# A written-out instruction schedule for attention plus gated MLP: a planner that counts DMA lanes and port locks, a new order of the first steps, and four fp32 matmul passes replaced by GpSimd subtractions

## The chip, the cores and the metric

One core of one Trainium2 chip runs the whole program. The metric is device time in microseconds (us). Five engines work side by side: TensorE (PE, with its weight loads PEld), VectorE (DVE), ScalarE (ACT), GpSimd (POOL) and SyncE (SP), which here only issues DMAs.

## The reference, cut to what matters

```python
# attention within chunks of 64 tokens; B, H, S, D = 8, 8, 576, 64
scores = (q_c @ k_c^T) / 8 ; attn = exp(scores - max) ; attn /= sum(attn) + 1e-9
x = (attn @ v_c), heads side by side            # (8, 576, 512), fp32
# gated MLP
h = gelu_tanh(x @ w_in)                         # w_in is 512 x 1024
u, v = h[..., :512], h[..., 512:]
v_n = (v - mean(v)) / sqrt(var(v) + 1e-6) * g_ln
v_s = einsum('ts,bsd->btd', w_sg, v_n) + b_sg   # over the 576 tokens
out = x + (u * v_s) @ w_out                     # w_out is 512 x 512
```

`w_in` and `w_out` arrive as float64 values, each as two 32-bit words, and are turned into fp32 pairs on the chip.

## The kernel before, in words

Every large product is done in three fp32r passes: each operand is split into a high part (rounded to fp32r) and a low part (what the rounding left), and low x high, high x low and high x high are added up in PSUM. So each weight and each activation passes through a split: a copy to the high part on ACT and a subtraction for the low part on DVE or POOL.

The work goes by batch (8) in units. `v_unit(b, m)` makes 128 tokens of v (12 matmuls of 512 columns), then gelu on ACT, statistics on DVE, the power -0.5 on POOL, and the split of the normalized v. `u_unit(b, dt)` makes 128 columns of u (24 matmuls of 288 columns). `s_unit` mixes tokens by w_sg and multiplies by u. The output product is `o_unit` in the first two batches and `o_fast` (seven half-size products) from batch 2 on. Between these stand the attention tiles (128 tokens each): `att_scores` (steps S and P), `att_transpose` (T), `att_out` (O and Q); the tiles below 5 go by `first_scores` and `first_out`.

The weights are prepared at the start. A quarter of `w_in` (512 columns of words) is loaded by `v_w_load` or `u_w_load` (steps L and, from within, w), taken apart by `pair_begin` (steps W and X: mostly DVE bit operations) and made into a high and a low part by `pair_end` (steps w and x). `pair_end` writes the high part with ACT, then adds in PSUM four passes over 512 columns: the fp32 value times an fp32 identity, two bf16 passes with the remaining bits of the float64 value, and the high part times the fp32r identity; ACT copies the sum to the low part. `w_out` is prepared in eight pieces of 256 columns by `o_w` (steps Y): `double_begin` has two two-input operations (multiply, add) by the engine `pick("Z")`, `double_end` one subtraction by `pick("Y")`. `pick(step)` gives GpSimd where the name is in `ON_POOL`, VectorE otherwise. The same tuple says, as `l0` to `l3`, for which of the first attention tiles `keep` makes the low part on POOL from a copy in SBUF, rather than on DVE from PSUM.

Nothing is issued where it is written. `Recorder` collects every operation into a `Plan`, so all of them bear line 224 in the profile and have to be told apart by their tiles. `Plan.emit` finds the true dependences, simulates the engines three times with the prices of `Op.price` (`run`; due times from `due`), and then issues every operation in the order of the planned start times. Each engine executes its own list strictly in order. TensorE may be planned out of the written order within a window of 96 operations (`AHEAD`); other engines take, of what can start within 200 ns, what is due first. The string `START` is the written order for batches 0 and 1 and for all weights; a letter is a step and the number its tile. It sets which TensorE work stands first, and by that all due times. Four scratch buffers of the tag `tmp` are shared by `hs`, `blocks`, `ot` and `r`, so an `ot` that waits for its output DMA can hold up any of the others.

Of the kernel before, what the change touches and what calls it, by code (L numbers as in the profile page):

```python
# [11 lines left out]
F32 = mybir.dt.float32  # L12
# [6 lines left out]
ALU = mybir.AluOpType  # L19
# [4 lines left out]
P = 128  # L24
DM = 512
DF = 1024
DH = DF // 2
# [15 lines left out]


START = """
L0 A0 B0 A1 B1 L1 S0 L2 T0 D11 A2 W0 A3 W1 L3 A4 S1 W2 S2 w0 w1 W3 T1 O0 w2 S3 O1 T2 w3 D14 O2 T3 S4 M0 v00 X0 O3 G0 T4
v01 A8 B8 O4 x0 X1 v02 x1 X2 v03 X3 v04 U0 x2 g0 g1 U1 x3 g2 g3 g4 F0 u02 F1 P5 u03 T5 s00 T6 P7 s01 Q5 s02 T7 T8
s03 Q7 v10 v11 Y0 v12 Y1 v13 Y2 u10 Y3 u11 Y4 u12 Y5 Y6 u13 Y7 A10 B10 s10 s11 P9 A12 s12 s13 T9 o00 T10 P11 A14
o01 o02 o03 Q9 B12 T11 o10 T12 o11 Q11 B14 S13 A15 o12 T13 o13
"""  # L50

SUMS = {5: 0, 6: 1, 7: 2, 8: 3}
# [14 lines left out]
}  # L67


ON_POOL = ("l0", "l1", "l2", "l3", "n2")  # L70
ACT_SOFTMAX = (0, 2, 4)


# [5 lines left out]
G_BLOCK = {(0, 0): 0, (1, 0): 1, (1, 1): 2, (0, 1): 3}  # L79


ENGINES = ("tensor", "vector", "scalar", "gpsimd", "sync")
AHEAD = 96
WAIT = {"tensor": 100, "gpsimd": 120}
# [33 lines left out]
class Op:  # L118
    def __init__(self, engine, method, args, kwargs):
        self.engine, self.method, self.args, self.kwargs = engine, method, args, kwargs  # L120
        outs = [kwargs["out"] if "out" in kwargs else args[0]]
        ins = [a for a in (*args[("out" not in kwargs):], *kwargs.values()) if is_ap(a)]
        ins = [a for a in ins if a is not kwargs.get("out") and a is not kwargs.get("accum_out")]
        self.outs, self.ins = outs + [a for a in [kwargs.get("accum_out")] if a is not None], ins
        self.deps, self.succ, self.tiles = set(), [], []
        self.table = next((TABLES.get(f, 0) for f in (*args, *kwargs.values()) if isinstance(f, AF)), 0) if engine == "scalar" else 0
        self.cost, self.lag = self.price()

    def price(self):

        n = max(a.free_size() for a in self.outs[:1] + self.ins[:2])
        psum = any(a.space == PSUM for a in self.outs + self.ins)
        if self.engine == "tensor":
            x = self.ins[-1]
            n = self.outs[0].free_size()
            if x.dtype == F32R:
                return 4.6 + 0.447 * n, 160
            if x.dtype == BF16:
                return 4.6 + 0.42 * n, 160
            if self.ins[0].ap[0][1] == D:  # L140
                return 39, 160
            return (115 if self.method == "transpose" else 1.76 * n + 10), 160
        if self.engine == "sync":
            size = self.ins[0].size() * 4
            return (460 if self.ins[0].ap[-1][1] >= P else 640), 2000 + size / 400
        if self.engine == "vector":
            one = len(self.ins) == 1 and not psum and self.method in ("tensor_copy", "tensor_scalar")
            return 75 + (0.53 if one else 1.04) * n, 80
        if self.engine == "scalar":
            return 100 + 0.82 * n + (100 if len(self.outs) > 1 else 0), 100  # L150
        return (850 if "pow" in str(self.kwargs.get("op")) else 200 + 1.8 * n), 42
# [10 lines left out]
class Plan:  # L162
# [82 lines left out]
    def run(self, users, after, at):  # L245
        ops = self.ops
        late = self.due(users, after, at)
        left = [len(op.deps) for op in ops]
        ready = [0.0] * len(ops)
        done = [None] * len(ops)  # L250
        start = [None] * len(ops)
        free = dict.fromkeys(ENGINES, 0.0)
        count = {t: len(u) for t, u in users.items()}
        gone = dict.fromkeys(users, 0.0)
        slots = {key: [0.0] * n for key, n in self.room.items()}
        key_of = self.tag_of
        tensor = [k for k, op in enumerate(ops) if op.engine == "tensor"]
        pe, table, wire = 0, 0, 0.0
        open_ = {e: {k for k, op in enumerate(ops) if op.engine == e and not left[k]} for e in ENGINES}

        def begin(k):
            op = ops[k]
            if left[k]:
                return None
            t = ready[k]
            for name in op.tiles:
                if count[name] < len(users[name]):
                    continue
                key = key_of[name]
                rank = 0 if name == next(n for n in self.order[key] if count[n] == len(users[n])) else 1  # L270
                if len(slots[key]) <= rank:
                    return None
                t = max(t, sorted(slots[key])[rank] + WAIT.get(op.engine, 33))
            return max(t, free[op.engine])

        for _ in range(len(ops)):
            best = None
            for e in ENGINES:
                if e == "tensor":
                    while pe < len(tensor) and start[tensor[pe]] is not None:  # L280
                        pe += 1
                    ks = [k for k in tensor[pe : pe + AHEAD] if start[k] is None]
                else:
                    ks = open_[e]
                found = [(b, k) for k in ks if (b := begin(k)) is not None]
                if not found:
                    continue
                t0 = min(found)[0]
                if e == "tensor":
                    t, k = min(found)  # L290
                    if best is None or t < best[0]:
                        best = (t, k)
                    continue
                t, k = min(
                    (late[k] + (1300 if ops[k].table not in (0, table) else 0), b, k) for b, k in found if b <= t0 + 200
                )[1:]
                if best is None or t < best[0]:
                    best = (t, k)
            t, k = best
            op = ops[k]  # L300
            e = op.engine
            if e != "tensor":
                open_[e].discard(k)
            start[k] = t
            cost = op.cost
            if e == "scalar" and op.table not in (0, table):
                table = op.table
                cost += 1200
            free[e] = t + cost
            done[k] = t + cost + op.lag  # L310
            if e == "sync":
                wire = max(t + 2000, wire) + op.lag - 2000
                done[k] = wire
            for name in op.tiles:
                if count[name] == len(users[name]):
                    slots[key_of[name]].remove(min(slots[key_of[name]]))
                count[name] -= 1
                gone[name] = max(gone[name], done[k])
                if not count[name]:
                    slots[key_of[name]].append(gone[name])  # L320
            for s in op.succ:
                left[s] -= 1
                if e != "tensor" or ops[s].engine != e:
                    ready[s] = max(ready[s], done[k] + WAIT.get(ops[s].engine, 33))
                if not left[s] and ops[s].engine != "tensor":
                    open_[ops[s].engine].add(s)
        return start
# [14 lines left out]
def block_attention_gated_mlp(ctx: ExitStack, tc: tile.TileContext, qkv, w_in, w_out, w_sg, g_ln, b_sg, out):  # L342
    nc = Plan(tc.nc)
# [25 lines left out]
    ident_r = const.tile([P, P], F32R, name="ident")  # L369
# [62 lines left out]
        q, lw, top = words[:, :n], words[:, 1::4], p.bitcast(U16)[:, 1::2]  # L432
        nc.vector.scalar_tensor_tensor(q, lw, 9, top, op0=ALU.logical_shift_right, op1=ALU.bitwise_or)

    def pair_end(n, hi, lo, st):

        f = st[:, 2 * n : 3 * n].bitcast(F32)
        p, q = st[:, 3 * n : 4 * n].bitcast(BF16)[:, 1::2], st[:, : 2 * n].bitcast(BF16)[:, :n]
        ps = ps_m.tile([P, 2, 512], F32, name="pm")[:, 0, :n]
        shape = lambda a: a.rearrange("p (k c) -> p k c", k=hi.shape[1]) if len(hi.shape) == 3 else a  # L440
        nc.scalar.mul(hi, shape(f), -1.0)
        terms = [(ident, f), (low[0], q), (low[1], p), (ident_r, hi)]
        for i, (a, c) in enumerate(terms):
            out_ps = shape(ps) if c is hi else ps
            nc.tensor.matmul(out_ps, a, c, start=(i == 0), stop=(i == len(terms) - 1))
        nc.scalar.mul(lo, shape(ps), -1.0)

# [8 lines left out]
        return a.rearrange("p (n k e) -> p n k e", n=n, k=2)  # L456

    staged = {}

    def v_w_begin(kt):  # L460

        pair_begin(DH, staged["v", kt])

    def v_w_end(kt):
        pair_end(DH, win_h[:, kt, DH:], win_l[:, kt, DH:], staged["v", kt])
        u_w_load(kt)

    def v_w_load(kt):
# [11 lines left out]

    def u_w_end(dt):
        cols = slice(dt * P, (dt + 1) * P)
        pair_end(DH, win_h[:, :, cols], win_l[:, :, cols], staged["u", dt])

    def o_w(et, half):
        nonlocal wout_h, wout_l
# [359 lines left out]
    held = {}  # L846
# [250 lines left out]
```

## Time and profile before

| | |
|---|---|
| median of 3 runs | 511.3 us (511.25 to 512.17) |
| profiled execution: time, span | 512.99 us, 511.2 us |
| PE busy | 493.0 us, 96% |
| DVE busy | 390.7 us, 76% |
| ACT busy | 288.8 us, 57% |
| POOL busy | 80.8 us, 16% |

Busy times are shares of the span of one execution. PE's ends are modelled, so a gap between two matmuls shows only where it is longer than the pipeline that the model adds. Times of rows are us from the start of the span, or ns where marked.

### The profile page before, as it was taken

To read this page: it belongs to the slowest core of one execution; us is meant where nothing else is said; L and a number is where in the kernel's file an instruction comes from. 1 tells how busy PE (TensorE), PEld (TensorE's weight loads), DVE (VectorE), ACT (ScalarE), POOL (GpSimd) and SP (SyncE) were. 2 spreads that over 40 slices of the span, in tenths; PEclk is the share of its full clock that TensorE was granted. 3 is DMA by queue.
4 is the path that set the end of the run, shared out by engine and by line. 5 is a ranking of instruction groups with operands and counts; after the bars stand their busy time and mean duration, and the time that the engine had idled before them with its cause. 6 is when DMAs were issued, how large, how long until landed. Compare 5 with 4: busy or idle time off the path is not lost.

```text
span 511.2 us, 12425 instructions
## 1 busy us (share of the span) xinstructions
PE 493.0 (96%) x5201; PEld 453.9 (89%) x5206; DVE 390.7 (76%) x719; ACT 288.8 (57%) x493; POOL 80.8 (16%) x83
## 2 busy tenths in 40 slices
PE   7899999999997989999999999999999999999996
PEld 5667898799987889998999899998999899998996
DVE  6889879898966697698758697698758797577056
ACT  5788667844434868439642578439642578313120
POOL 0122200220510241011200141011200131002000
PEclk9999999999998999999999999999999999999999
DMA  8984011223245422414120504415120501020002
GB/s 330 356 188 150 0 44 42 85 84 124 65 132 161 140 52 74 126 56 136 38 73 25 169 22 108 126 65 138 30 71 24 172 19 27 1 71 24 1 1 92
DMA packets 52683, 46.58 MB, mean 91 GB/s; under 512 B 35218, under 2 KB 45458, under 8 KB 52628
## 3 DMA queue, kind: packets, MB, share of 16 engines
q1 hardware_dynamic: 52628, 45.80, 29.8%
q8 instruction: 41, 0.67, 0.6%
q14 instruction: 14, 0.11, 0.1%
HBM read 36.34 MB, written 9.44 MB: 90 GB/s over the span
## 4 chain that ended last, share of the span: by engine, by line
PE 56%; DVE 24%; ACT 11%; issue 3%; DMA 2%; POOL 1%; SPq 1%; DVEq 0%; POOLq 0%; ACTq 0%
PE pm L224 55%; DVE nmax L224 5%; ACT ptT L224 3%; DVE sm L224 2%; DVE pt L224 2%; DVE st L224 2%; DVE blocks L224 2%; DVE hs L224 2%; ACT L224 2%; ACT z L224 2%; DVE v L224 1%; ACT xf L224 1%; PE banks L224 1%; ACT pt L224 1%; DVE gl L224 1%
## 5 line engine op out<-in xcount | busy, mean ns | idle before, releaser
L224 PE MATMUL pm<-wsg,v 128*128 128x288 f32 x768 | 108.1, 296 | 0.4 <-issue 0.4
L224 PEld LDWEIGHTS pm<-wsg,v 128*128 128x128 f32 x768 | 103.9, 188 | 0.9 <-issue 0.5
L224 ACT COPY ptT<-blocks 32x256 f32<-32x256 f32 (+1 forms) x93 | 44.2, 476 | 34.2 <-DVE blocks L224 32.0
L224 POOL TENSOR_TENSOR sm<-sm,neg_half 128x1 f32<-128x1 f32 x36 | 31.0, 863 | 197.7 <-DVE sm L224 193.5
L224 PE MATMUL pm<-xh,win_l 128*128 128x288 f32 x256 | 55.6, 299 | 0.0
L224 PE MATMUL pm<-xh,win_h 128*128 128x288 f32 x256 | 55.0, 296 | 0.0
L224 PE MATMUL pm<-xl,win_h 128*128 128x288 f32 x256 | 55.0, 296 | 0.0
L224 PE MATMUL pm<-gh,wout 128*128 128x288 f32 x272 | 54.0, 300 | 0.0
L224 PE MATMUL pm<-win_h,xl 128*128 128x512 f32 x128 | 51.7, 404 | 0.0
L224 POOL TENSOR_TENSOR pt<-pt,nmax 128x512 f32<-128x512 f32 x27 | 30.2, 1132 | 131.5 <-DVE nmax L224 126.1
L224 PE MATMUL pm<-win_h,xh 128*128 128x512 f32 x128 | 50.9, 397 | 0.0
L224 PE MATMUL pm<-win_l,xh 128*128 128x512 f32 x128 | 50.7, 396 | 0.0
L224 ACT CAST gh<-u 128x576 fp32r<-128x576 f32 x32 | 21.4, 673 | 48.9 <-DVE u L224 48.8
L224 ACT ACT_TABLE_LOAD x32 | 41.1, 1283 | 9.0 <-DVE pt L224 7.7
L224 PEld LDWEIGHTS pm<-gh,wout 128*128 128x128 f32 x272 | 43.3, 192 | 0.3
L224 DVE TENSOR_TENSOR u<-pm,u 128x576 f32<-128x576 f32 x32 | 24.1, 753 | 24.7 <-PE pm L224 24.5
L224 PEld LDWEIGHTS pm<-xh,win_l 128*128 128x128 f32 x256 | 41.4, 188 | 1.3
L224 PEld LDWEIGHTS pm<-xl,win_h 128*128 128x128 f32 x256 | 41.1, 188 | 0.0
L224 PEld LDWEIGHTS pm<-xh,win_h 128*128 128x128 f32 x256 | 41.0, 188 | 0.0
L224 ACT ACTIVATE hs<-pm 128x512 f32<-128x512 f32 x36 | 21.3, 596 | 27.1 <-PE pm L224 23.0
L224 PE MATMUL pm<-gl,wout 128*128 128x288 f32 x136 | 35.8, 300 | 0.0
L224 DVE BATCH_NORM_STATS2 sm<-hs 128x6 f32<-128x512 f32 x36 | 24.7, 686 | 10.8 <-ACT hs L224 10.7
(126 smaller groups left out, 955.3 us busy)
## 6 DMA issues: line engine op xcount, KB each, us to landing
qk<-qkv SPq DMA_DIRECT2D x31, 512.0 KB, 4.7
out_dram<-ot SPq DMA_DIRECT2D x31, 288.0 KB, 2.2
av<-qkv SPq DMA_DIRECT2D x116, 64.0 KB, 3.3
wsg<-w_in SPq DMA_DIRECT2D x4, 512.0 KB, 7.6
wout<-w_in SPq DMA_DIRECT2D x4, 512.0 KB, 8.0
st<-w_out SPq DMA_DIRECT2D x8, 256.0 KB, 3.0
qkv_w<-qkv SPq DMA_DIRECT2D x2, 768.0 KB
stage<-w_sg SPq DMA_DIRECT2D x5, 288.0 KB, 3.8
```

Of the source, the lines that this page charges most:

```text
L224: getattr(getattr(self.nc, op.engine), op.method)(*op.args, **op.kwargs)
```

## The change

1. `START` is another order of the same steps; among the differences, the loads come as `A1 L2 L0 ...`, `U1` stands before `U0`, the pieces `Y` lie differently among `u1x` and `s1x`, and at the end of batch 1 `Q11` (the attention output of tiles 11 and 12) stands behind `o12 T13` instead of ahead of `B14`.
2. `ON_POOL` becomes `("Y", "Z", "l0", "l2", "l3", "n2")`: the three two-input operations of each of the eight `w_out` pieces move from DVE to POOL, and the low part of attention tile 1 moves from POOL to DVE.
3. `pair_end` gets an engine. For the four u parts of `w_in` (`REST_U = "gggg"`), POOL subtracts the high part from the fp32 value, and the fp32 pass over the identity goes; for the v parts nothing changes.
4. The planner's prices are set anew, a DMA waits for the oldest of eight lanes, and a DVE operation and a POOL operation that both lock are not planned side by side.

```diff
-L0 A0 B0 A1 B1 L1 S0 L2 T0 D11 A2 W0 A3 W1 L3 A4 S1 W2 S2 w0 w1 W3 T1 O0 w2 S3 O1 T2 w3 D14 O2 T3 S4 M0 v00 X0 O3 G0 T4
-v01 A8 B8 O4 x0 X1 v02 x1 X2 v03 X3 v04 U0 x2 g0 g1 U1 x3 g2 g3 g4 F0 u02 F1 P5 u03 T5 s00 T6 P7 s01 Q5 s02 T7 T8
-s03 Q7 v10 v11 Y0 v12 Y1 v13 Y2 u10 Y3 u11 Y4 u12 Y5 Y6 u13 Y7 A10 B10 s10 s11 P9 A12 s12 s13 T9 o00 T10 P11 A14
-o01 o02 o03 Q9 B12 T11 o10 T12 o11 Q11 B14 S13 A15 o12 T13 o13
+A1 L2 L0 A0 B0 B1 L1 S0 T0 A2 A4 W0 A3 D11 W1 L3 S1 W2 S2 S3 w0 w1 W3 T1 O0 w2 O1 T2 w3 D14 T3 S4 M0 O2 v00 X0 O3 G0
+T4 v01 A8 B8 O4 x0 X1 v02 x1 X2 v03 U1 X3 v04 U0 x2 g0 P5 x3 g2 g3 g4 F0 u02 g1 F1 u03 T5 s00 T6 P7 s01 Q5 s02 T7 T8
+s03 Q7 v10 v11 Y0 v12 v13 Y2 Y1 u10 Y3 u11 Y4 s10 Y5 s11 Y6 u13 Y7 u12 A10 B10 s12 P9 A12 s13 T9 T10 o02 P11 A14 o01
+o03 o00 Q9 B12 T11 o10 T12 o11 B14 S13 A15 o12 T13 Q11 o13
-ON_POOL = ("l0", "l1", "l2", "l3", "n2")
+ON_POOL = ("Y", "Z", "l0", "l2", "l3", "n2",)
+REST_V, REST_U = "pppp", "gggg"
...
         if self.engine == "sync":
-            size = self.ins[0].size() * 4
-            return (460 if self.ins[0].ap[-1][1] >= P else 640), 2000 + size / 400
+            return (420 if self.ins[0].ap[-1][1] >= P else 620), 2500 + self.ins[0].size() / 100
+        wide = [a for a in self.ins if a.free_size() > 1]
+        copies = self.method in ("tensor_copy", "tensor_scalar") and n > 1
+        if self.engine == "gpsimd":
+            self.locks = self.method == "tensor_tensor" and n > 8
         if self.engine == "vector":
+            self.locks = not psum and (len(wide) > 1 or copies)
...
+            if op.engine == "sync":
+                t = max(t, lanes[0])
+            if op.locks:
+                a, b = held["gpsimd" if op.engine == "vector" else "vector"]
+                if a <= t < b:
+                    t = b
...
         terms = [(ident, f), (low[0], q), (low[1], p), (ident_r, hi)]
+        if eng is not None:
+            eng.tensor_tensor(lo, shape(f), hi.bitcast(F32), op=ALU.add)
+            terms = [(low[0], q), (low[1], p), (ident_r, lo)]
```

## Rows read from the trace of the kernel before

**Rows 1.** Page, part 1: busy time, share of the span, instructions of each engine.
```profile
PE 493.0 (96%) x5201; PEld 453.9 (89%) x5206; DVE 390.7 (76%) x719; ACT 288.8 (57%) x493; POOL 80.8 (16%) x83
```

**Rows 2.** Busy time by stretch: length, each engine's busy us (instructions), clock, DMA, GB/s.
```profile
0.00:36.00 36.00, 29.24 (x369) 21.55 (x374) 28.74 (x59) 25.58 (x83) 5.60 (x10) 1.00 0.96 308
36.00:66.00 30.00, 30.00 (x267) 24.36 (x265) 25.71 (x50) 22.88 (x41) 6.37 (x7) 1.00 0.23 68
66.00:130.00 64.00, 63.11 (x646) 58.84 (x645) 58.42 (x124) 40.51 (x68) 9.22 (x9) 1.00 0.24 75
130.00:160.00 30.00, 26.15 (x370) 24.86 (x372) 21.89 (x37) 11.37 (x20) 7.79 (x6) 1.00 0.39 119
160.00:226.00 66.00, 64.20 (x740) 59.50 (x733) 52.64 (x95) 42.63 (x63) 12.22 (x13) 0.97 0.33 95
226.00:340.50 114.50, 113.93 (x1268) 107.24 (x1267) 88.72 (x159) 68.00 (x101) 17.90 (x18) 1.00 0.30 84
455.20:511.20 56.00, 51.89 (x354) 49.47 (x352) 27.57 (x47) 12.10 (x19) 3.75 (x4) 1.00 0.11 38
```

**Rows 3.** Waits of PE from 0 to 36: who for whom, us in total, times, longest.
```profile
PE pm L224 <- ACT ident L224: 2.4, 1, 2.4
PE pm L224 <- DVE wout L224: 1.2, 1, 1.2
PE pm L224 <- DVE wsg L224: 1.0, 1, 1.0
PE banks L224 <- ACT first_ptT L224: 0.7, 1, 0.7
PE banks L224 <- ACT xf L224: 0.7, 1, 0.7
PE pm L224 <- DVE first_pts L224: 0.6, 1, 0.6
```

**Rows 4.** Timeline 138 to 160: who waits before the longest pause of PE (in brackets).
```profile
146.16 5.82 SPq L224 DMA_DIRECT2D av<-qkv  x8
...
152.08 2.52 SPq L224 DMA_DIRECT2D out_dram<-ot  x2
...
153.72 0.69 PE L224 MATMUL pm<-qk 64*64 64x64 f32 x32 [1.17 <-DVE xl L224]
...
157.85 0.76 DVE L224 TENSOR_TENSOR ot<-pm,xf 128x576 f32<-128x576 f32 x1 [2.52 <-DMA out_dram<-ot]
...
158.64 0.60 DVE L224 COPY ptT<-blocks 32x256 f32<-32x256 f32 x2
159.02 0.30 PE L224 MATMUL pm<-ptT,av 64*64 64x64 f32 x2 [2.69 <-issue]
```

**Rows 5.** PE by stretches of 3 us there: length, busy (instructions), granted clock.
```profile
156.00:159.00 3.00, 0.33 (x3) 1.00 0.43 81
159.00:162.00 3.00, 2.98 (x40) 0.66 0.84 282
162.00:165.00 3.00, 3.00 (x20) 0.77 0.40 91
165.00:168.00 3.00, 3.00 (x20) 1.00 0.27 101
```

**Rows 6.** Timeline around the last of the four fp32 passes, PE's matmuls: start, us, instructions.
```profile
58.92 0.43 PE L224 MATMUL pm<-xh,win_h 128*128 128x288 f32 x2
...
59.19 1.02 PE L224 MATMUL pm<-wout,ident 128*128 128x512 f32 x2
...
60.05 0.60 PE L224 MATMUL pm<-wout,low 128*128 128x512 bf16 x2
```

**Rows 7.** Timelines: PE, the first of the four passes; DVE, the last part's last bits.
```profile
38.60 1.02 PE L224 MATMUL pm<-wsg,ident 128*128 128x512 f32 x2
...
46.99 0.69 DVE L224 SCALAR_TENSOR_TENSOR wout<-wout 128x512 uint16<-128x512 uint16 x1
```

**Rows 8.** Groups by form: the DVE operations that move, and POOL's and DVE's kinds like them.
```profile
L224 DVE TENSOR_TENSOR st<-st 128x256 f32<-128x256 f32 x16 | 6.7, 422 | 0.4
L224 DVE TENSOR_TENSOR wout<-st,wout 128x256 fp32r<-128x256 f32 x8 | 3.4, 421 | 0.5 <-ACT wout L224 0.5
L224 POOL TENSOR_TENSOR pt<-pt,nmax 128x512 f32<-128x512 f32 x27 | 30.2, 1132 | 131.5 <-DVE nmax L224 126.1 <-ACT hs L224 2.8 <-DVE sm L224 2.7
L224 POOL TENSOR_TENSOR xl<-xf,xh 128x512 fp32r<-128x512 f32 x4 | 5.7, 1420 | 26.0 <-ACT xh L224 26.0
L224 POOL MEMSET eye<- 128x128 f32 x1 | 0.2, 205 | 0.3 <-POOLq L1086 0.3
L224 DVE SCALAR_TENSOR_TENSOR wsg<-wsg 128x512 int32<-128x512 int32 x4 | 2.8, 693 | 0.1
L224 DVE TENSOR_TENSOR xl<-pm,xh 128x512 fp32r<-128x512 f32 x28 | 18.3, 687 | 14.8 <-ACT xf L224 13.4 <-ACT xh L224 1.4
```

**Rows 9.** Timeline, DVE beside POOL: first of eight lengthened DVE operations before 160 us.
```profile
16.75 1.27 POOL L224 TENSOR_TENSOR xl<-xf,xh 128x512 fp32r<-128x512 f32 x1 [15.46 <-ACT xh L224]
16.82 1.75 DVE L224 SCALAR_TENSOR_TENSOR wout<-wout 128x512 int32<-128x512 int32 x1
```

**Rows 10.** Timeline 134.5 to 137, DVE and POOL: the last of the eight.
```profile
135.21 1.81 POOL L224 TENSOR_TENSOR r<-r 128x512 f32<-128x512 f32 x1
135.87 1.29 DVE L224 COPY ptT<-blocks 32x256 f32<-32x256 f32 x1
```

**Rows 11.** Timeline of PE, 28 to 28.6: the first matmul of a v unit.
```profile
28.46 0.50 PE L224 MATMUL pm<-win_h,xl 128*128 128x512 f32 x1
```

More of the change, by code (lines that the diff above doesn't have):

```diff
@@ L126, in __init__ @@
         self.table = next((TABLES.get(f, 0) for f in (*args, *kwargs.values()) if isinstance(f, AF)), 0) if engine == "scalar" else 0
+        self.locks = False
         self.cost, self.lag = self.price()
@@ L136, in price @@
             if x.dtype == F32R:
-                return 4.6 + 0.447 * n, 160
+                return (5.9 if n < 400 else 4.6) + 0.447 * n, 160
             if x.dtype == BF16:
@@ L140, in price @@
             if self.ins[0].ap[0][1] == D:
-                return 39, 160
-            return (115 if self.method == "transpose" else 1.76 * n + 10), 160
+                return 40, 160
+            return (118 if self.method == "transpose" else 1.83 * n + 10), 160
         if self.engine == "sync":
-            size = self.ins[0].size() * 4
-            return (460 if self.ins[0].ap[-1][1] >= P else 640), 2000 + size / 400
+            return (420 if self.ins[0].ap[-1][1] >= P else 620), 2500 + self.ins[0].size() / 100
[3 more added lines that the diff above has]
+            self.locks = self.method == "tensor_tensor" and n > 8
         if self.engine == "vector":
+            if self.method == "memset":
+                return 600, 80
+            self.locks = not psum and (len(wide) > 1 or copies)
             one = len(self.ins) == 1 and not psum and self.method in ("tensor_copy", "tensor_scalar")
@@ L254, in run @@
         gone = dict.fromkeys(users, 0.0)
+        heads = {key: list(names) for key, names in self.order.items()}
         slots = {key: [0.0] * n for key, n in self.room.items()}
@@ L257, in run @@
         tensor = [k for k, op in enumerate(ops) if op.engine == "tensor"]
-        pe, table, wire = 0, 0, 0.0
+        pe, table, wire, lanes = 0, 0, 0.0, [0.0] * 8
+        held = {"vector": [0.0, 0.0], "gpsimd": [0.0, 0.0]}
         open_ = {e: {k for k, op in enumerate(ops) if op.engine == e and not left[k]} for e in ENGINES}
@@ L269, in begin @@
                 key = key_of[name]
-                rank = 0 if name == next(n for n in self.order[key] if count[n] == len(users[n])) else 1
+                rank = 0 if name == heads[key][0] else 1
                 if len(slots[key]) <= rank:
@@ L273, in begin @@
                 t = max(t, sorted(slots[key])[rank] + WAIT.get(op.engine, 33))
-            return max(t, free[op.engine])
+            t = max(t, free[op.engine])
+            if op.engine == "sync":
[4 more added lines that the diff above has]
+                    t = b
+            return t
         for _ in range(len(ops)):
@@ L311, in run @@
             if e == "sync":
-                wire = max(t + 2000, wire) + op.lag - 2000
+                wire = max(t + 2500, wire) + op.lag - 2500
                 done[k] = wire
+                lanes.append(wire)
+                del lanes[0]
+            if op.locks:
+                held[e] = [t, t + cost + op.lag]
             for name in op.tiles:
@@ L316, in run @@
                     slots[key_of[name]].remove(min(slots[key_of[name]]))
+                    heads[key_of[name]].remove(name)
                 count[name] -= 1
@@ L433, in pair_begin, with pair_end @@
         nc.vector.scalar_tensor_tensor(q, lw, 9, top, op0=ALU.logical_shift_right, op1=ALU.bitwise_or)
-    def pair_end(n, hi, lo, st):
+    def pair_end(n, hi, lo, st, eng):
         f = st[:, 2 * n : 3 * n].bitcast(F32)
@@ L442, in pair_end @@
         terms = [(ident, f), (low[0], q), (low[1], p), (ident_r, hi)]
+        if eng is not None:
+            eng.tensor_tensor(lo, shape(f), hi.bitcast(F32), op=ALU.add)
+            terms = [(low[0], q), (low[1], p), (ident_r, lo)]
         for i, (a, c) in enumerate(terms):
-            out_ps = shape(ps) if c is hi else ps
+            out_ps = shape(ps) if c is hi or c is lo else ps
             nc.tensor.matmul(out_ps, a, c, start=(i == 0), stop=(i == len(terms) - 1))
@@ L458, in block_attention_gated_mlp @@
     staged = {}
+    REST = {"p": None, "v": nc.vector, "g": nc.gpsimd}
     def v_w_begin(kt):
@@ L464, in v_w_end @@
     def v_w_end(kt):
-        pair_end(DH, win_h[:, kt, DH:], win_l[:, kt, DH:], staged["v", kt])
+        pair_end(DH, win_h[:, kt, DH:], win_l[:, kt, DH:], staged["v", kt], REST[REST_V[kt]])
         u_w_load(kt)
@@ L482, in u_w_end @@
         cols = slice(dt * P, (dt + 1) * P)
-        pair_end(DH, win_h[:, :, cols], win_l[:, :, cols], staged["u", dt])
+        pair_end(DH, win_h[:, :, cols], win_l[:, :, cols], staged["u", dt], REST[REST_U[dt]])
     def o_w(et, half):
```

## The prediction

> **What bounds the kernel now.** I read the page's busy times first, then busy time by stretch, then the timeline at each stretch where PE is not full. PE is busy for 493.0 of 511.2 us [rows 1], so a gain has to come either from less PE work or from the 18.2 us in which PE stands still. The stretches say where those lie [rows 2]: 6.8 us before 36 us, none from 36 to 66, 0.9 from 66 to 130, 3.9 from 130 to 160, 1.8 from 160 to 226, then 0.6 in 114 us and 4.1 at the end (the last results on their way out, which the change leaves alone). From 226 us on PE sets the pace and a better plan has almost nothing to win; what can move lies in the first 226 us.
>
> In the first 36 us PE waits 2.4 us for the identity, which stays, and 4.2 us in five waits for DVE and ACT work on the first tiles and on the v parts of w_in [rows 3]; the 16 DMA engines are busy for 0.96 of that time [rows 2], so part of this is set by data arriving, and part by DVE, busy for 28.7 of 36 us.
>
> The pause at 159 us is one mechanism that the reader can follow [rows 4]. SP issues eight loads of v tiles in 5.8 us, and two output DMAs stand behind them until 152.08. The `ot` buffers that they empty come free late, so DVE waits 2.52 us with its next `ot` at the head of its list; the half-done `ptT` copies of an attention tile stand behind it on DVE and are done from 158.94 on; PE, which has that tile's output next, starts at 159.02 after 2.69 us. Another 1.17 us goes at 153.72. After the pause the granted clock is 0.66 for 3 us and 0.77 for the next 3, and 1.00 again [rows 5]: in part at the lower level, 1.2 GHz instead of 2.4. That is 3 x 0.34 + 3 x 0.23 = 1.71 us more. The place costs 1.17 + 2.69 + 1.71 = 5.57 us.
>
> **Part 1, the fp32 pass.** An fp32 pass over 512 columns is two matmuls; the last of the four begins at 59.19 and the bf16 pass behind it at 60.05 [rows 6], so it takes 0.86 us of PE's line. The first of the four begins at 38.60 [rows 7]. Four go: 4 x 0.86 = 3.44 us. PE is full from 36 to 66 [rows 2], so this shortens its line by that much there. What takes its place is a POOL subtraction of 512 columns, 1.13 to 1.42 us by kinds of the same width [rows 8], between ACT's high part and the last PE pass. Queued behind it on POOL are the power operations of the v units; for these DVE, then ACT wait. PE has v units of other tiles to do meanwhile, and the bits of the last u part, which DVE finishes 0.69 us after 46.99 [rows 7], waited for a pass at 59.19, so I cost the added latency at nothing; without that cover it is up to 1.42 us for each part, 5.7 in all.
>
> **Part 2, w_out on POOL.** Twenty-four DVE operations of 0.42 us go [rows 8]: 16 x 0.422 + 8 x 0.421 = 10.1 us, in a stretch in which DVE is busy for 58.4 of 64 us [rows 2]. Tile 1's low part comes to DVE for 0.69 us [rows 8]. The trace has no POOL two-input operation of 256 columns. From below half of 1.13, 0.57 us; from above the whole, 1.13. POOL's small memset takes 0.21 [rows 8], so the fixed part can't be large: 0.21 + 0.92 / 2 = 0.67 us, an estimate. So POOL gets 24 x 0.67 = 16.1 us, and four subtractions at 1.42 make 21.8; tile 1's 1.28 leaves it: 20.5 net. POOL itself has room, 15.6 of 94 us busy from 36 to 130 [rows 2].
>
> The price is on DVE. A DVE operation that usually takes 0.69 us [rows 8] took 1.75 when it began 0.07 us after a POOL one of 1.27 [rows 9]: it ran when POOL had ended. Eight DVE operations before 160 us are lengthened this way, the first in [rows 9] and the last in [rows 10], by 7.0 us in all, beside 15 POOL operations of 512 columns with 20.5 us: 0.34 us of DVE for each us of POOL. At that rate the added POOL time costs DVE 0.34 x 20.5 = 7.0 us, and DVE is better off by 10.1 - 0.7 - 7.0 = 2.4 us. The bounds are no waiting (9.4 us better) and all of it (11.1 worse). I take DVE as even for PE's line: its relief lies behind a PE that was full there anyway.
>
> The Trainium skill, page "SBUF — State Buffer", section "SBUF: two separate sides", speaks against this move: it says that VectorE operations with two SBUF inputs and GpSimd operations take one shared pair of ports as an exclusive lock, and the one that comes second is blocked for the whole of the other. The 1.75 us of [rows 9] agrees. By that rule moving work to POOL frees no DVE time where DVE wants the ports at every moment; that is the third rival below, whose sum is the one by this rule at its worst; at the trace's rate it is the forecast's.
>
> **Part 3, the planner and the order.** Q11 now stands behind o12 and T13. That gives PE a whole o unit before the tile whose `ptT` came late: 24 matmuls, at 0.13 us each (the two of 288 columns from 58.92 to 59.19 in [rows 6]) 3.2 us, against the 2.69 it waited [rows 4]. PE also arrives 3.4 us earlier, DVE no later. I take the place at 153 to 163 as gone: -5.57, the half clock with it. At worst nothing of it goes, or another pause of this size stands elsewhere. The DMAs count too: the eight loads still hold SP for 5.8 us, and an output that is made earlier can still be issued behind them. What is late next is the run of DVE and ACT work from 160 to 226, where DVE is busy for 52.6 of 66 us and PE loses 1.8 [rows 2]; with PE earlier I let that loss happen a second time: +1.8. For the start I take 0, between the 4.2 us of waits that a good order could remove [rows 3] and as much again that a bad one could add. New prices alone, in the steady stretch, are worth at most its 0.6 us per 114.
>
> **Sum.** On the profiled execution, 512.99 us (span 511.2 and 1.8 around it): -3.44 - 5.57 + 1.8 + 0 + 0 = -7.2, which makes 505.8. This execution stands 1.7 above the median of the runs, so on that scale 511.3 - 7.2 = 504.1.
>
> **Rivals.**
> - *A wait takes the place of the pass* (no change, 511.3; 510 to 512.5). PE gives up 3.44 us by 66 us and gets them back as a longer wait at 153, because SP's loads and the `ot` buffers set that time. For it: the wait there is on a DMA, not on PE. Against: the steps on both sides of it have been reordered, and that DMA's input is made by PE.
> - *Everything that waits goes* (499.0): also three quarters of the 4.2 us in the start, 3.2, and the 1.8 isn't lost again: 511.3 - 3.44 - 5.57 - 3.2 = 499.1. For it: the lanes are counted where DMA is fullest. Against: what the data rate sets no order removes.
> - *The ports make DVE the bound* (slower, 514). Every added us of POOL blocks DVE: DVE gets 11.1 us more between 36 and 130. Its idle time there is 4.3 + 5.6 = 9.9 us [rows 2], but half of that stands where it waits for PE or ACT; 5 absorbed leave 6.1: 511.3 - 3.44 + 6.1 = 514.0, with the pause at 159 still there. It decides from the point where over 9.4 / 20.5 = 0.46 of POOL's time blocks DVE; it was 0.34. A planner that sees the locks speaks against it, DVE's 58.4 busy us of 64 from 66 to 130 for it. It is what the lock in the Trainium skill's page "SBUF — State Buffer" (section "SBUF: two separate sides") would do at its worst.
> - *The order doesn't do what it says:* PE's window of 96 operations lets the planner put Q11's matmuls where they were. Then only the passes go and the 1.8 isn't lost: 511.3 - 3.4 = 507.9. I count this in the forecast's own range.
>
> **How the numbers follow.** Forecast 0.50 (own range 500.5 to 508.5), no change 0.17, everything 0.15, slower 0.18. A measurement of this kernel tells 0.2%, some 1 us, from no change. Faster: 0.50 + 0.15 and half of the no-change case, 0.08, so 0.73; same 0.08; slower 0.19 with a little of that case. The range takes all of the forecast and most of the no-change and the better case: 498.5 to 512.5.
>
> **What would show it.** Eight PE matmul records fewer; no `wsg,ident` or `wout,ident` row behind 36 us; the S units of batch 0 some 3 us earlier. No PE wait over 1 us and a full clock from 130 to 170. DVE's `st` and `wout` sums gone, and its lengthened operations beside POOL at some 0.34 of POOL's added time. The steady stretch of 114.5 us unchanged. The forecast is wrong if a PE wait of several us stands anywhere between 36 and 226, above all one with a lowered clock behind it, or if the first v unit starts later than before, 28.46 us [rows 11].

## The result, and the profile after

The changed kernel takes 504.5 us (median of 4 runs, 503.9 to 504.6) against 511.7 beside it (511.3 to 512.6): ratio 0.985, 95% interval 0.984 to 0.987, faster by some 7.3 us. Forecast were 504.1 us and a gain of 7.2. The number came out; half of its working did not, as the experiments show, and that the errors cancel is luck.

The page's first part (busy us, share, instructions) and the busy times of the changed kernel by the stretches of [rows 2] (length, busy us per engine, granted clock, DMA, GB/s):

```profile
PE 487.9 (97%) x5198; PEld 451.6 (90%) x5198; DVE 383.6 (76%) x696; ACT 288.5 (57%) x493; POOL 107.1 (21%) x110
```

```profile
0.00:36.00 36.00, 29.03 (x389) 22.03 (x390) 27.57 (x61) 26.38 (x84) 6.41 (x10) 1.00 0.90 306
36.00:66.00 30.00, 27.22 (x224) 22.05 (x223) 28.22 (x49) 20.89 (x38) 12.20 (x10) 0.94 0.30 87
66.00:130.00 64.00, 63.84 (x658) 60.41 (x657) 53.38 (x102) 39.99 (x70) 31.12 (x35) 1.00 0.22 67
130.00:160.00 30.00, 30.00 (x417) 29.07 (x416) 26.25 (x45) 16.04 (x27) 8.52 (x7) 1.00 0.43 136
160.00:226.00 66.00, 65.14 (x795) 59.90 (x797) 51.86 (x94) 43.75 (x65) 11.07 (x11) 1.00 0.33 98
226.00:340.50 114.50, 114.35 (x1306) 107.69 (x1299) 88.23 (x159) 68.41 (x103) 18.23 (x18) 1.00 0.30 84
```

Three things are to be seen beside [rows 2]. From 130 to 160 PE is full, where it lost 3.85 us, and the clock stays at 1.00 through 226. From 36 to 66, where PE was full, it now stands still for 2.78 us, the clock is 0.94 (30 x 0.06 = 1.8 us more), and DVE's busy time has grown from 25.71 to 28.22 of 30. The steady stretch is as before.

So the first matmul of batch 0's S units comes later, not earlier, although four passes less lie ahead of it. PE's timeline of the kernel before, then of the changed one (start, us, instructions):

```profile
68.40 0.83 PE L224 MATMUL pm<-wsg,v 128*128 128x288 f32 x5
```

```profile
70.26 3.35 PE L232 MATMUL pm<-wsg,v 128*128 128x288 f32 x24
```

The waits of PE behind this, 36 to 66 us, and the granted clock around the longer one:

```profile
PE pm L232 <- ACT u L232: 1.9, 1, 1.9
PE pm L232 <- ACT hs L232: 0.8, 1, 0.8
```

```profile
54.00:57.00 3.00, 1.09 (x7) 1.00 0.00 0
57.00:60.00 3.00, 3.00 (x17) 0.60 0.00 0
60.00:63.00 3.00, 3.00 (x71) 0.83 0.00 0
```

Where this pause comes from can be followed on the timelines of POOL, DVE, ACT and PE, here from 49 to 57 us (in brackets: idle time before it, and what ended it):

```profile
49.10 1.55 POOL L232 TENSOR_TENSOR win_l<-wout,win_h 128x512 fp32r<-128x512 f32 x1 [2.38 <-ACT win_h L232]
52.81 2.33 POOL L232 TENSOR_TENSOR sm<-sm,neg_half 128x1 f32<-128x1 f32 x1 [2.16 <-DVE sm L232]
```

```profile
49.39 1.87 DVE L232 TENSOR_TENSOR wsg<-stage,wsg 128x576 fp32r<-128x576 f32 x1
...
52.65 0.74 DVE L232 SCALAR_TENSOR_TENSOR hs<-hs,sm,g_bc 128x512 f32<-128x512 f32 x1
53.31 1.41 DVE L232 TENSOR_TENSOR wsg<-stage,wsg 128x576 fp32r<-128x576 f32 x2
```

```profile
55.17 0.72 ACT L232 ACTIVATE v<-hs,sm 128x512 fp32r<-128x512 f32 x1 [3.72 <-POOL sm L232]
55.80 0.63 ACT L232 ACTIVATE u<-pm 128x576 f32<-128x576 f32 x1
```

```profile
56.48 0.54 PE L232 MATMUL pm<-xh,win_l 128*128 128x288 f32 x2 [1.91 <-ACT u L232]
```

The new POOL subtraction for the last u part starts at 49.10; a w_sg split on DVE, usually 0.75 us, begins 0.29 us later and takes 1.87. All of DVE's list behind it is late, with it the sum that POOL's power operation needs. That operation, on one column, starts at 52.81, beside three DVE operations in a row that each read two tensors of SBUF, and takes 2.33 us where its mean is 0.94: some 1.3 us more than in the other places where it was begun beside such an operation (0.92 to 1.02 between 40 and 66 us), so this wait is the larger part of the pause. ACT has the v scaling that needs it at the head of its list and the first u gelu behind; the gelu empties the PSUM buffer that PE waits for.

### The profile page after: what moved, and what is told of

Same layout as the page of the kernel before. It is cut to its first block, busy times and chain, and to the rows that moved or that the text cites. A ratio compares the mean times of both kernels' runs of the same rounds, so it can differ in the third digit from the quotient of the medians.

```text
span 502.7 us, 12445 instructions
## 1 busy us (share of the span) xinstructions
PE 487.9 (97%) x5198; PEld 451.6 (90%) x5198; DVE 383.6 (76%) x696; ACT 288.5 (57%) x493; POOL 107.1 (21%) x110
## 4 chain that ended last, share of the span: by engine, by line
PE 66%; DVE 16%; ACT 9%; DMA 4%; issue 3%; POOL 1%; SPq 0%; DVEq 0%; POOLq 0%; ACTq 0%
PE pm L232 66%; DMA qk<-qkv 2%; DVE nmax L232 2%; ACT L232 2%; DVE u L232 2%; DVE wsg L232 1%; DVE sm L232 1%; ACT pt L232 1%; DMA wout<-w_in 1%; DVE v L232 1%; DVE xl L232 1%; ACT ptT L232 1%; DVE gl L232 1%; DVE hs L232 1%; DVE wout L232 1%
## 5 line engine op out<-in xcount | busy, mean ns | idle before, releaser
L232 POOL TENSOR_TENSOR sm<-sm,neg_half 128x1 f32<-128x1 f32 x36 | 33.9, 942 | 166.0 <-DVE sm L232 164.8
L232 ACT ACTIVATE v<-hs,sm 128x512 fp32r<-128x512 f32 x32 | 23.0, 723 | 20.1 <-POOL sm L232 15.8
```

Of the source, the lines that this page charges most:

```text
L232: getattr(getattr(self.nc, op.engine), op.method)(*op.args, **op.kwargs)
```

## The experiments

Times stand beside runs of the kernel before on the same chip, where its median was 512.8 to 513.0; a ratio is to those. Each edit is to the changed kernel, or, where it says so, to the kernel before. "Order kept" means that every engine issues its list in the order of the changed kernel's plan, so that only the edit differs; "planned anew" means that the planner made new lists for the edited program.

**The changed kernel itself**, on the chip of the last runs:

> The changed kernel itself, beside the others on one chip. Every theory: the same pause of PE at 54 to 57 us; 504 to 506 us, the ratio to before 0.982 to 0.988.

504.1 us, ratio 0.984 (0.981 to 0.986), with the same pause.

**The four passes put back, order kept.**

```diff
+        if eng is not None:
+            nc.before[len(nc.ops)] = lambda: tc.nc.tensor.matmul(ps, ident, f, start=True, stop=True)
...
+                if k in self.before:
+                    self.before[k]()
```

> The changed kernel with its planned order kept as it is, but for each of the four u parts of w_in one fp32 pass over 512 columns is issued on TensorE again, just ahead of the first bf16 pass, into the same PSUM bank (the bf16 pass overwrites it, so nothing else changes). Theory (the four passes lay on PE's line, 0.86 us each): 504.5 + 3.4 = 507.9 us, 507.2 to 508.6. Rival (the change's new pause of PE at 54 to 57 us, or waits for ACT and POOL before it, take the passes in): 504.5 to 505.5.

503.4 us, ratio 0.982 (0.978 to 0.985): not slower with 3.4 us more of PE work, and below even the rival's times. Its busy times from 36 to 66:

```profile
36.00:66.00 30.00, 29.57 (x241) 22.95 (x237) 28.77 (x50) 22.12 (x44) 10.80 (x10) 1.00 0.30 89
```

The clock stays at 1.00. The total refutes my theory's time, but not all of its mechanism. The four passes, then the power operation with the three DVE operations around it, and PE's start behind its only wait in this stretch:

```profile
39.60 1.02 PE L472 MATMUL pm<-wsg,ident 128*128 128x512 f32 x2
45.19 1.02 PE L472 MATMUL pm<-wsg,ident 128*128 128x512 f32 x2
59.41 1.02 PE L472 MATMUL pm<-wout,ident 128*128 128x512 f32 x2
62.13 1.12 PE L472 MATMUL pm<-wout,ident 128*128 128x512 f32 x2
```

```profile
53.61 0.73 DVE L235 SCALAR_TENSOR_TENSOR hs<-hs,sm,g_bc 128x512 f32<-128x512 f32 x1
53.77 0.99 POOL L235 TENSOR_TENSOR sm<-sm,neg_half 128x1 f32<-128x1 f32 x1 [2.17 <-DVE sm L235]
54.27 1.41 DVE L235 TENSOR_TENSOR wsg<-stage,wsg 128x576 fp32r<-128x576 f32 x2
...
56.11 0.54 PE L235 MATMUL pm<-xh,win_l 128*128 128x288 f32 x2 [0.43 <-ACT u L235]
```

Set against the profile of the changed kernel operation by operation, PE is 0.92 us late before the first pass, from the start, and 1.11 late at the end of its work before the pause: the waits took in all but 0.2 of the first two passes' 1.72 us. The last two, behind the pause, put PE back by 1.8 us, their full price. What pays for that is not the passes' doing as far as the rows show: the power operation takes 0.99 us here and 2.33 in the changed kernel, beside the same three DVE operations and begun as long after the first of them (0.16 us). That is 1.34 of the 1.48 us by which the pause is shorter, and with it the lowered clock is gone, another 1.5 us before the last two passes begin. PE's first S matmul starts at 70.17, against 70.26. So in this run two of the four passes were on the path; why the power operation waits less here is open.

**The passes back, planned anew** (`REST_U = "pppp"`):

> The changed kernel with the four fp32 passes in place of GpSimd's subtractions, planned anew. Theory (between 36 and 66 us VectorE, not PE, sets the pace as soon as the passes go, so they cost nothing): PE full from 36 to 66, no lowered clock there, VectorE's lengthened operations there fewer by some 3.3 us, time within 1 us of the changed kernel or below it, 502.5 to 505.5. Rival (the passes are worth their 3.4 us and only this order's pause hides it): 506.5 to 509.

503.5 us, ratio 0.983 (0.981 to 0.985). PE is full again, though DVE is still busy for 28.63 us of this stretch:

```profile
36.00:66.00 30.00, 29.72 (x239) 23.42 (x238) 28.63 (x50) 22.94 (x40) 8.06 (x8) 1.00 0.30 88
```

DVE's lengthened operations there fall from 4.4 us to 2.5 by their rows, less than the 3.3 expected. The theory's result holds: without the part of the change that removes the passes, the other parts give the whole gain. The power operation took 0.93 us in this run, with no pause of PE behind it, so this run does not tell what the subtractions cost from what that operation's wait costs.

**The subtraction alone, in the kernel before** (four lines of `pair_end`, GpSimd for the u parts):

> The kernel before, planned by its old planner and in its old order, with GpSimd's subtraction in place of the four fp32 passes and nothing else. Theory (at this place the passes are worth their 3.4 us only if no new wait takes them; the pause at 153 to 163 stays as it is): 507.9 to 509.5 us with the pause at 153 still there. Rival (a new pause between 40 and 60 us with a lowered clock takes it all): 511 to 513.

513.0 us, ratio 1.000 (0.997 to 1.003): the rival, at its word. A pause of PE appears at 45 us, with a lowered clock behind it; the one at 153 is shorter but there. PE's waits of over 1 us from 36 to 66 and from 130 to 170, and the clock after the first:

```profile
PE pm L224 <- ACT hs L224: 2.4, 2, 1.8
```

```profile
PE pm L224 <- ACT ptT L224: 1.3, 1, 1.3
PE pm L224 <- DVE xl L224: 1.2, 1, 1.2
```

```profile
47.00:51.00 4.00, 4.00 (x13) 0.57 0.02 4
```

**The subtractions on VectorE, order kept.**

```diff
+                rest = op.engine == "gpsimd" and op.outs[0].tensor.name.startswith("win_l")
-                getattr(getattr(self.nc, op.engine), op.method)(*op.args, **op.kwargs)
+                getattr(getattr(self.nc, "vector" if rest else op.engine), op.method)(*op.args, **op.kwargs)
```

> The changed kernel with its planned order kept, but the four subtractions of the u parts of w_in run on VectorE (0.69 us each, 2.8 in all) at their places in the order. Theory (GpSimd's subtractions cost VectorE more than they spare it: three of them hold up one VectorE operation each by 1.1 us, 3.3 in all, and the last one delays the w_sg splits ahead of the pause): PE's pause at 54 to 57 us is shorter by 0.5 us or more and the clock stays up; 502 to 504. Rival (VectorE is the full engine here and 2.8 us more of it delays all): the pause grows, 505 to 507.

502.2 us, ratio 0.980 (0.978 to 0.983), the fastest version run; on the same chip the changed kernel stood at 504.1, though the two intervals overlap. DVE around the last subtraction (compare 49.10 to 51.26 above), then the power operation, and PE's first clock row after its pause:

```profile
48.69 0.69 DVE L233 TENSOR_TENSOR win_l<-wout,win_h 128x512 fp32r<-128x512 f32 x1
49.30 0.75 DVE L233 TENSOR_TENSOR wsg<-stage,wsg 128x576 fp32r<-128x576 f32 x1
```

```profile
51.66 2.26 POOL L233 TENSOR_TENSOR sm<-sm,neg_half 128x1 f32<-128x1 f32 x1 [6.42 <-DVE sm L233]
```

```profile
56.00:59.00 3.00, 3.00 (x24) 1.00 0.00 0
```

On DVE the subtraction takes 0.69 us and blocks nothing; the pause is 1.27 us in place of 1.91, and the clock stays at 1.00. DVE's lengthened operations from 34 to 66 us fall from 4.4 us to 1.1 by their rows, so 2.8 us of work replace 3.3 of waiting. The power operation still takes 2.26 us: its wait does not need a subtraction on POOL. Of the 2.0 us much is the clock: the mean granted clock was 1.000 in the four executions from 501.9 to 502.3 us, and in two of the changed kernel's six on that chip, which took 502.1 and 503.4 us; its other four had 0.992 to 0.998.

**The same, planned anew** (`REST_U = "vvvv"`):

> The same four subtractions on VectorE, planned anew by the new planner. Theory: as with the order kept, 501.5 to 504, since the planner can also place them. Rival: the new order brings a pause of its own with a lowered clock, 505 to 508.

508.0 us, ratio 0.992 (0.990 to 0.994): the rival. The plan has a pause of its own at 38 us, with a lowered clock:

```profile
PE banks L232 <- DVE first_pts L232: 3.1, 1, 3.1
```

The same edit is worth -2.0 us with one order and +3.8 with another.

**ScalarE's gelu ahead of the v scaling, order kept otherwise** (one operation moved one place):

> The changed kernel with its planned order kept, but on ScalarE the first u gelu of batch 0 stands ahead of the v scaling that it follows in the plan. Theory (PE's pause at 54 to 57 us is ScalarE's list standing behind a power operation on GpSimd that waits for the shared ports): the gelu runs by 55.4, PE waits some 1.1 us less, the clock stays at 1.0, and the time is 501.5 to 503.0 us. Rival (the gelu waits itself, for the w_sg splits on VectorE that free its tile, until 55.5 or later): no change, 504 to 505, the clock lowered again.

503.8 us, ratio 0.983 (0.978 to 0.987): in the theory's clock, but not below its upper end. PE's wait for the gelu shrinks from 1.9 to 0.3 us and the clock stays up from 36 to 66; most of the time then goes to the next wait:

```profile
PE pm L238 <- ACT win_l L238: 1.3, 1, 1.3
...
PE pm L238 <- ACT u L238: 0.3, 1, 0.3
```

From the changed kernel's 504.1 this can't be told apart.

**w_out's operations back on VectorE, order kept** (POOL's two-input operations of 256 columns issue on DVE):

> The changed kernel with its planned order kept, but the 24 two-input operations of 256 columns of the w_out pieces run on VectorE again, each at the same place in the order. Theory (about even for PE: the port lock takes back what VectorE is spared): 504 to 505.5 us, DVE's lengthened operations between 75 and 130 us nearly gone. Rival A (VectorE's relief is what removed the pause of PE at 153 to 163 us): that pause comes back, 508 to 510. Rival B (the ports cost more than the move spares): 502 to 503.5.

507.3 us, ratio 0.989 (0.985 to 0.993): 3 us slower, in rival A's direction but short of its 508 to 510, and in another place: there is no pause at 153 but one at 89 us, behind a DVE list that is too long, with a clock of 0.97 over 66 to 130. Against the second profiled execution of the changed kernel the span is 506.0 to 503.0 us: the 1.5 of this pause and 1.7 of clock.

```profile
PE pm L233 <- DVE ptT L233: 1.5, 1, 1.5
```

**The new GpSimd list alone, in the kernel before:**

> The kernel before with the new list of what runs on GpSimd alone (w_out's two-input operations to GpSimd, tile 1's low part to VectorE), old planner, old order, fp32 passes kept. Theory (VectorE's relief from 65 to 130 us is what removes the pause at 153 to 163 us): no PE wait over 1 us there, 505.5 to 507.5 us. Rival A (the ports take it back): 510 to 513 with the pause in place. Rival B (the pause only moves, earlier or later): 508 to 511.

512.7 us, ratio 0.999 (0.997 to 1.002): rival A's time with rival B's mechanism. From 130 to 170 PE loses 1.12 us, where the kernel before loses 3.85, and no wait there is over 1 us. DVE's busy time from 66 to 130 falls from 58.42 to 48.76 us, but the old plan lets PE pause at 88 us, and the clock is low for the 6 us behind it:

```profile
PE pm L224 <- DVE ptT L224: 2.0, 1, 2.0
```

```profile
90.00:96.00 6.00, 6.00 (x51) 0.50 0.22 63
```

**The old START string:**

> The changed kernel with the old START string, planned anew with the new planner. Theory (Q11 behind o12 and T13 removes the pause of PE at 153 to 163 us, worth 5.6): the pause and its lowered clock are back, 508.5 to 511. Rival A (the planner's DMA lanes and locks remove it): no pause there, 503.5 to 506. Rival B (the order of the first steps also cost the new pause at 54 to 61 us): that one goes with the old string, 4.4 less, and the sum is about even at 504 to 506 with the pause at 153 present.

505.9 us, ratio 0.987 (0.983 to 0.991): rival A. With Q11 in its old place the pause at 153 does not come back, PE being busy for 29.58 us from 130 to 160:

```profile
130.00:160.00 30.00, 29.58 (x410) 28.37 (x409) 22.76 (x39) 13.48 (x23) 8.60 (x8) 1.00 0.44 132
```

**The old planner:**

> The changed kernel with the planner of before (old prices, no DMA lanes, no locks), all else new. Theory (the order string, the passes and the w_out move make the gain; the planner little): 503.5 to 506.5. Rival A (the lanes let the output DMAs go before the v loads, and without them PE's pause near 153 us is back): 508 to 511. Rival B (locks unseen, VectorE is blocked at bad moments between 36 and 130): new PE waits there, 506.5 to 509.

510.6 us, ratio 0.996 (0.993 to 0.998): the planner is worth some 6.4 us in this kernel. No pause at 153 either, but two of over 2 us before it, rival B and at more than its price, each with a lowered clock:

```profile
PE pm L226 <- ACT hs L226: 2.3, 1, 2.3
PE pm L226 <- DVE v L226: 2.1, 1, 2.1
```

```profile
48.00:51.00 3.00, 2.84 (x8) 0.63 0.02 5
113.00:117.00 4.00, 4.00 (x21) 0.58 0.01 2
```

**The new planner alone, in the kernel before:**

> The kernel before with the new planner alone (prices, DMA lanes, locks); old order string, old list for GpSimd, fp32 passes kept. Theory (the planner gives few microseconds in this order, and the pause at 153 is the w_out work's): 509 to 512 us, pause present. Rival (the planner removes the pause by itself): 504.5 to 507, no PE wait over 1 us between 130 and 165.

510.4 us, ratio 0.997 (0.994 to 1.000): the theory's time, the rival's mechanism. From 130 to 170 PE loses 0.55 us and the pause is gone, but 1.7 us are lost at 185, and in the start the clock was 0.91, worth over 3 us. That is not the old string's doing by itself: the run above with the same string and planner had 1.00 there. The two quickest executions, 508.6 and 509.0 us, had a mean clock of 0.997, the others 0.990 to 0.993:

```profile
0.00:36.00 36.00, 28.82 (x346) 20.78 (x347) 26.75 (x56) 24.32 (x68) 5.82 (x10) 0.91 0.87 300
...
130.00:170.00 40.00, 39.45 (x552) 37.00 (x551) 30.25 (x55) 18.89 (x34) 5.66 (x5) 1.00 0.42 126
```

## Why the prediction was right, and where it was not

**The passes, -3.44: wrong.** The work went, the time did not. The step that failed is the one that costs POOL's latency "at nothing" because PE has other v units to do. PE was full from 36 to 66 in [rows 2], but DVE was close behind it, 25.71 of 30, and POOL's subtractions made it 28.22: three of them hold up one DVE operation each by 1.1 us, 3.3 in all. PE waits 2.7 us and pays 1.8 in clock: 4.5 against 3.44. I had this as the first rival, in the wrong place (at 153, not at 54).

How the 4.5 divide is shown in part. With the subtractions on VectorE and the order kept, the pause is 0.64 us shorter. The power operation's long wait is another 1.3 us, and it does not come from subtractions on POOL alone: it took 2.26 us without them, and 0.99 with them in the run with the passes. Of the passes themselves, put back with the order kept, the first two were covered by waits and the last two, 1.8 us, were on PE's line. With the passes planned anew the sum comes out the same, 503.5 against 504.1; the subtractions on VectorE planned anew settle nothing, since that plan has a pause of its own.

**The port lock: near in sum, wrong in place.** I priced 7.0 us of waiting, 0.34 us of DVE for each us of POOL, from all of the first 160 us. Counted by their rows in the same way, DVE's lengthened operations there went from 7.0 to 12.3 us, 5.3 more. But beside the u subtractions it is 3.3 us for 6.1 us of POOL, 0.54, in a stretch in which DVE was busy for 28.22 of 30. The Trainium skill, page "SBUF — State Buffer", section "SBUF: two separate sides", says that the one that comes second is blocked for the whole of the other; DVE's 1.87 us at 49.39 agrees. I had not priced the other direction at all: the power operation's 2.33 us, which goes beyond that sentence, since it sat out three DVE operations and not one.

**The w_out move: even for PE was too low.** With the order kept it is worth 3 us, 1.7 of them the clock. POOL's operations of 256 columns took 0.77 us, estimated at 0.67, in a stretch in which DVE's busy time fell from 58.42 to 53.38:

```profile
L232 POOL TENSOR_TENSOR st<-st 128x256 f32<-128x256 f32 x16 | 12.4, 775 | 30.9 <-DVE st L232 21.4 <-ACT hs L232 8.9
L232 POOL TENSOR_TENSOR wout<-st,wout 128x256 fp32r<-128x256 f32 x8 | 6.2, 771 | 4.3 <-ACT wout L232 4.3
```

"Its relief lies behind a PE that was full there anyway" overlooked that PE is full there only as long as DVE keeps up: with these operations back on VectorE it waits 1.5 us at 89, for a `ptT` copy late on DVE's list.

**The pause at 153 to 163, -5.57: right in size, its cause wrong.** It is gone: 3.85 us of idle time and the 1.7 of clock. But Q11's new place did not do it: with the old string and all else new it is gone, and with the new planner alone in the old kernel too; with the new GpSimd list alone no wait of over 1 us is left there. In the changed kernel SP still issues eight loads in 5.77 us ahead of an output:

```profile
146.71 5.77 SPq L232 DMA_DIRECT2D av<-qkv  x8
152.57 0.55 SPq L232 DMA_DIRECT2D out_dram<-ot  x1
```

Only one output stands behind them there, where two did in [rows 4], and no `ot` on DVE waits for a buffer. By these runs it was a coincidence of lists, which any of several other plans avoids.

**160 to 226, +1.8: wrong sign.** PE's idle time there went from 1.80 to 0.86. The loss that I let return did not; a larger one, with another cause, stands 100 us earlier.

**The start, 0: right.** 6.97 us without PE before 36, against 6.76. The first v unit starts at 31.25, 2.8 us later than in [rows 11], which I had named as a sign of being wrong; but 24.28 us of PE's work now lie ahead of it, against 22.37. The other sign, a wait with a lowered clock behind it between 36 and 226, did come, at 54.

**The scale: 1.7 us that the median does not hold.** The sum takes 1.71 us of lowered clock off 511.3. On the chips of the experiments the kernel before took 510.5 to 511.8 us in 14 executions with a mean granted clock of 1.000, and 511.8 to 515.3 in 33 with 0.988 to 0.997. The profiled one, 512.99 at 0.997, is of the second kind; a time of 511.3 lies among the first, which have no such loss to give back. The same terms then make 505.8 on either scale. The changed kernel has losses of its own: 0.995 to 0.997 in all four executions of the result. At 1.000, on the last chip, it took 502.1 and 503.4 against 510.8 to 511.8: some 8 us.

In idle time and clock together: +4.6 from 36 to 66, -0.7 to 130, -3.9 to 160, -2.9 to 226 (of that 66 x 0.03 = 2.0 the clock), and -3.4 of work: -6.3. The profiled span fell by 8.5; the other 2.2 lie behind 226 us, where 0.9 less is idle, or in the distances between matmuls that count as busy, and were not followed.

**What the gain is made of.** The single parts in the old kernel give 0.0 (subtraction), -0.3 (w_out) and -2.5 us (planner); taken from the changed kernel they cost -0.7, 3.2, 6.4, and the order string 1.8. They don't add up: each alone has pauses of its own in its profile, and most of these a lowered clock. That the planner with the locks and lanes is what lets the relief of DVE arrive at PE fits these numbers and is not shown. Which of prices, lanes and locks does it was not tried one by one, and the order string alone in the old kernel neither.

## What to carry to other kernels

An engine that is full is the bound only as long as the next one behind it has room: before work is taken off it, sum the busy time of the engine that feeds it in the same 30 us, and add what the replacement costs that engine through shared ports. Test a part with the order of issue frozen as well as with a new plan; the same edit gave -2.0 and +3.8 us here, and only the frozen run tells its price. Read even that run operation by operation, and not by its total: the run with the passes paid 2.0 us for them and won 3.0 by a shorter pause and a full clock, and its total showed neither. A right total with wrong terms is found only by putting each term back.

## What the runs showed of the hardware

- A pause of PE can cost more than its length, and its length alone does not tell whether it will. Behind the 1.9 us that end at 56.48 the granted clock was at its lower level for some 3.4 us, worth 1.7; the same was lost behind 1.5 us (w_out's operations on VectorE, at 89), 1.8, 2.1, 2.3 and 3.1, and twice as much behind 2.0 (the new GpSimd list alone). Behind 1.3 us (subtractions on VectorE, and the gelu moved), 1.7 (the planner alone, before 185) and 2.25 (the old START string, before 20) it stayed at 1.00. In two profiled executions of the changed kernel, each with a pause of 1.49 us near 10 us, it was 1.00 in one and 0.72 in the other. What decides, these runs do not show. Those two (length, busy us of PE, clock, DMA, GB/s):

```profile
9.00:15.00 6.00, 4.94 (x103) 1.00 1.02 405
9.00:15.00 6.00, 4.66 (x41) 0.72 1.02 404
```

- GpSimd's power operation on a single column waits for DVE too: from 40 to 66 us it took some 0.55 us beside DVE operations with one tensor input, 0.92 to 1.02 when begun beside one with two SBUF inputs, and 2.33 (four profiles; 2.26 in a fifth) when it sat out three in a row. In the run with the passes it took 0.99 beside the same three. What decides between the two is not shown.
